# The end of a cached-attention layer: one head's PV moved behind half of the last pair's PV, and two runs of matmuls rolled into loops

## The chip, the core and the metric

The kernel runs on one core of one Trainium2 chip. The metric is the device time of one execution in microseconds (us). The core has a matrix engine (PE, with its weight loads shown as PEld), a vector engine (DVE), an activation engine (ACT), GpSimd (POOL) and an engine that here only starts transfers (SP). Each engine works through its own list of instructions in order; they meet at semaphores.

## The reference, cut to what matters

Two equal layers follow each other for one new token of a batch of two. Each is an attention over a cache of 16384 positions in 32 heads, and then a small MLP:

```python
def _A_ref(x, k_cache, v_cache, wq, wo):          # caches: 2 x 32 x 16384 x 128, bf16
    q = (x @ wq) split into 32 heads of 128
    scores = einsum("bhqd,bhkd->bhqk", q, k_cache) * 128 ** -0.5
    o = einsum("bhqk,bhkd->bhqd", softmax(scores), v_cache)
    return o, heads side by side, @ wo            # wo: 4096 x 576
def _B_ref(x, w1, w2, w3, w4):                    # x: 2 x 1 x 576
    ...
    h2 = gelu(layernorm(x1) @ w3) @ w4            # w3: 576 x 4608, w4: 4608 x 576
x = x + _A_ref(layernorm(x), ...); x = x + _B_ref(layernorm(x), ...)      # twice
```

K and V of one batch element and head ("head" below; there are 64) are 4 MB each.

## The kernel before, in words

**Memory and transfers.** One SBUF array `mem` is cut into six slots of 32 KB per partition. `plan_all` writes down every transfer in the order in which SP starts them; `Store.pump` lets a transfer start only when the last reader of its place is done. Transfers are planned far ahead, so a long queue of them stands in front of the DMA engines.

**Attention.** Heads go in pairs (`pair`, `pair_end`): PE transposes half of K (L1324) and multiplies it by q (L1335), ACT copies the transposes (L1425), DVE does the other half of K by products and sums (L1347, L1350); then the maximum over all partitions on POOL (L1371), the exponentials on ACT, and the product of the probabilities with V, "PV", on PE: 256 matmuls of one 128-wide block each (L1402). The pairs of a layer run in a loop of the program on PE, ACT and DVE; a place that changes by turn (which slot K lies in) is addressed through a register, and a register instruction stands ahead of each transpose (L1324). Each loop's body is built to start at the head of a block of instructions (`head_slot`).

**Layer 1's end** (`attention`, its last branch). One single head `c` is left after the pairs, and the last pair's PV. In order: `q_row` and `single` (K of `c`: L1309, L1435 on PE, L1446 and L1449 on DVE), `softmax_max` (DVE, then POOL's reduction over the partitions, L1464), `softmax_exp` (ACT, L1474 and L1478), `pv` of `c` (128 matmuls, L1511, into column 448 of the PSUM tile `mps`, copied out by ACT, L1493). Then the last pair's PV in four quarters (`pv_pair_part`, L1402) into the same two columns; its V comes in two transfers of 4 MB, one for quarters 0 and 1, one for 2 and 3. Between the halves stands `totals` (L1231: sums over the softmax denominators). `weighted` (L1063) and a fold by PE (L1022) turn all heads' outputs into the operand of wo.

**Landings.** `landed` puts an item in POOL's list that waits for a transfer and then raises a semaphore that PE waits on. POOL works through its list in order, and the same list holds the reductions.

**After attention.** `rows_projection` multiplies by wo (32 rows of 5 matmuls in three pieces of 11, 11 and 10 rows, L924), then layernorms, w3 (L800, L817), gelu, w4 (L924 again, six pieces), and the output. SP's queue after the last pair's V holds, in this order, wo, w3, w4 and w1. Part of w4 goes to the slot in which V of head `c` lies.

Of the kernel before, what the change touches and what calls it, by code (L numbers as in the profile page):

```python
# [4 lines left out]
ACT = mybir.ActivationFunctionType  # L5
# [337 lines left out]
class KB:  # L343
# [346 lines left out]
    def layer(self, l):  # L690
        if l == 0:
            self.unscaled()
        self.q_projection(l)
        if l == 0:
            self.hs_projection()
            self.quads()
        self.attention(l)
        ot = self.otn.rearrange("p (b j) -> p j b", b=self.B)
        self.rows_projection("wo", l, lambda k: ot[:, k, :], "prod")
        self.add_psum(self.x, "x", self.x, "x", self.unscaled)  # L700
        self.layernorm("x", self.x, self.xb, "xb")
        self.dv(lambda e: e.tensor_copy(out=self.mean0[:, :], in_=self.mv[:, 0, :]), reads=["mv"], writes=["mean0"])
        self.dv(lambda e: e.tensor_copy(out=self.rstd0[:, :], in_=self.rstd[:, :]), reads=["rstd"], writes=["rstd0"])
        self.dv(lambda e: e.tensor_tensor(out=self.x1[:, :, :], in0=self.xb[:, :, :], in1=self.hs[:, :, :],
                                          op=ALU.add), reads=["xb", "hs"], writes=["x1"])
        self.z_projection(l)
        if l == 0:
            self.turn(1, settle=False)
        self.gelu_z()
        self.settle()  # L710
        self.rows_projection("w4", l, lambda k: self.gT[:, k * self.B:(k + 1) * self.B], "prod")
        self.dv(lambda e: e.tensor_tensor(out=self.x[:, :, :], in0=self.x[:, :, :], in1=self.x1[:, :, :],
                                          op=ALU.add), reads=["x", "x1"], writes=["x"])
        if l < self.NL - 1:
            self.add_psum(self.x, "x", self.x, "x", self.unscaled)
        else:
            self.dv(lambda e: e.tensor_tensor(out=self.xo[:, :, :], in0=self.x[:, :, :],
                                              in1=self.mps[:, 0:self.KT * self.B].rearrange("p (t b) -> p t b", b=self.B),
                                              op=ALU.add),
                    reads=["mps", "x"], writes=["xo"])  # L720
# [190 lines left out]
    def rows_projection(self, w, l, rhs, rk):  # L911

        KT, B, D = self.KT, self.B, self.D
        cuts = self.cuts[w, l]
        last = cuts[-1][1] - 1
        for i, (a, b, _) in enumerate(cuts):
            nm = (w, l, i)
            buf = self.store.buf(nm)

            def f(pe, a=a, b=b, buf=buf):  # L920
                for k in range(a, b):
                    for t in range(KT):
                        o = (k - a) * D + self.kcol[t]
                        ins = pe.matmul(self.mps[:, t * B:(t + 1) * B], lhsT=buf[:, o:o + 128], rhs=rhs(k),  # L924
                                        start=(k == 0 and t == 0), stop=(k == last), skip_group_check=True)
                return ins
            self.pe(f, reads=[rk] + self.store.keys(nm), writes=["mps"])
            self.store.release(nm)
            if (w, i) == ("w4", 2 - l):
                self.layernorm("xb", self.xb, self.xn2[:, l, :, :], "xn2", bank=self.BANK)  # L930
                if l == self.NL - 1:
                    self.gelu(self.eps, "eps", self.junk, "junk")
            if l == 0:
                self.turn(self.TURNS.get((w, i), 0))
# [38 lines left out]
    def attention(self, l):  # L973
        o = self.order(l)
        n = self.PAIRS[l]
        at = lambda i: 2 * i - 1 if l == 0 else 2 * i + 1
        self.l_now = l
        if l:
            self.carried(o)
        else:  # L980
            self.q_row(o[0], 0, 2)
            self.q_turn(o[1], None)
            self.single(o[0], 0, 2)
            self.softmax_max(o[0], 0, 2)
            self.softmax_exp(o[0], 0, 2)
            self.pv(l, o[0], 0)
        self.pair(l, o[at(1)], 0, None, 2 * l)
        first = self.g.mark()
        first.pop("vector")
        self.base = self.chunk  # L990
        self.pair_end(o[at(1)], o[at(2)])
        sums = self.g.mark()["vector"]
        for i in range(2, n):
            self.pair(l, o[at(i)], (i - 1) % 2, o[at(i - 1)])
            self.pair_end(o[at(i)], o[at(i + 1)])
        self.g.loop({"vector": sums}, n - 2)
        last = o[at(n)]
        self.pair(l, last, (n - 1) % 2, o[at(n - 1)])
        self.g.loop(first, n - 1)
        self.base = None  # L1000
        self.pair_end(last)
        c = o[-1]
        if l == 0:
            self.last_three(last, *o[-3:])
        else:
            self.q_row(c, 0, 2)
            self.single(c, 0, 2)
            self.softmax_max(c, 0, 2)
            self.softmax_exp(c, 0, 2)
            self.pv(l, c, 0)  # L1010
            self.landed("vp", last, apart=True)
            for g in range(4):
                if g == 2:
                    self.totals(l)
                self.pv_pair_part(l, last, g)
            for h in range(2):
                self.weighted(last + h, self.mps[:, 448 + h:449 + h])
        t = self.sps[self.BANK][:, self.U:2 * self.U]

        def f(pe):  # L1020
            for b in range(self.B):
                ins = pe.matmul(t[:, 32 * b:32 * b + 32], lhsT=self.spread[:, 128 * b:128 * (b + 1)],  # L1022
                                rhs=self.fold[:, :], start=True, stop=True, skip_group_check=True)
            return ins
        self.pe(f, reads=["prod", "fold"], writes=[("sps", self.BANK)])
        self.dv(lambda e: e.tensor_copy(out=self.otn, in_=t), reads=[("sps", self.BANK)], writes=["prod"])
# [456 lines left out]
                                            bias=self.ls[:, 1, z:z + 1]),  # L1483
                     reads=[("ls0", z), ("ls1", z)], writes=[("l", u)])

    def pv(self, l, u, z, land=True):

        if land:
            self.landed("v", u)
        n = self.BP // 2  # L1490
        for b in range(0, self.NB, n):
            self.pv_part(l, u, z, b, b + n)
        self.act(lambda e: e.activation(out=self.o_acc[:, u:u + 1], in_=self.mps[:, 448:449], func=ACT.Copy),  # L1493
                 reads=["ops"], writes=[("o", u)])

    def pv_part(self, l, u, z, b, end):

        p = self.p[z]
        runs = []
        while b < end:  # L1500
            nm = next(x for x in self.store.pieces("v", u) if x[2] <= b < x[2] + x[3])
            m = min(end, nm[2] + nm[3]) - b
            runs.append((b, m, *self.tile("v", u, b, m)))
            b += m
        keys = [k for r in runs for k in r[4]]

        def f(pe):
            for b0, m, _, buf, _ in runs:
                for j in range(m):
                    b = b0 + j  # L1510
                    ins = pe.matmul(self.mps[:, 448:449], lhsT=buf[:, j * 128:(j + 1) * 128], rhs=p[:, b:b + 1],  # L1511
                                    start=b == 0, stop=b == self.NB - 1, skip_group_check=True)
            return ins
        self.pe(f, reads=[("p", z), ("p2", z)] + [("landed", r[2]) for r in runs] + keys, writes=["ops"])
        for _, m, nm, _, _ in runs:
            self.used(l, nm, m)

# [92 lines left out]
```

## Time and profile before

| | us |
|---|---|
| median of 3 runs | 2540.45 (2539.97 to 2540.72) |
| the profiled execution's own time | 2540.23 |
| its span, first to last instruction | 2538.4 |
| busy: PE / PEld / DVE / ACT / POOL | 1621.6 / 1478.7 / 1881.7 / 1255.4 / 30.8 |
| read from HBM | 1091.46 MB, 430 GB/s over the span |

Times in a profile count from the span's start; 1.83 us of the execution's time lie outside the span. A row of the timeline gives start, duration, engine, line of the kernel, operation, output and inputs with their shapes, how many such instructions follow each other, and in brackets how long the engine stood idle before and what ended that. "issue" means that it waited for nothing that the profile shows. PEq, PEldq, DVEq and SPq are the engines' sequencers, which run register and branch instructions and start transfers.

### The profile page before, as it was taken

To read this page: it belongs to the slowest core of one execution; us is meant where nothing else is said; L and a number is where in the kernel's file an instruction comes from. 1 tells how busy PE (TensorE), PEld (TensorE's weight loads), DVE (VectorE), ACT (ScalarE), POOL (GpSimd) and SP (SyncE) were. 2 spreads that over 40 slices of the span, in tenths; PEclk is the share of its full clock that TensorE was granted. 3 is DMA by queue.
4 is the path that set the end of the run, shared out by engine and by line. 5 is a ranking of instruction groups with operands and counts; after the bars stand their busy time and mean duration, and the time that the engine had idled before them with its cause. 6 is when DMAs were issued, how large, how long until landed. Compare 5 with 4: busy or idle time off the path is not lost.

```text
span 2538.4 us, 82111 instructions
## 1 busy us (share of the span) xinstructions
PE 1621.6 (64%) x34342; PEld 1478.7 (58%) x34342; DVE 1881.7 (74%) x1549; ACT 1255.4 (49%) x1940; POOL 30.8 (1%) x94
## 2 busy tenths in 40 slices
PE   3665665666666666657667765666566666656666
PEld 3555655565556556556656655565566556555655
DVE  5877787787787777777648877877778778778773
ACT  2545545445446455455435564454554544644542
POOL 0000000000000000000000000000000000000000
PEclk8666666666666666666656666666666666666665
DMA  9999999999999999999999999999999999999999
GB/s 413 431 435 433 433 435 433 433 433 437 432 434 432 438 430 435 433 433 434 414 411 418 430 430 443 432 431 430 443 432 430 431 439 435 431 431 436 438 423 395
DMA packets 30226, 1092.31 MB, mean 430 GB/s; under 512 B 3284, under 2 KB 4440, under 8 KB 10840
## 3 DMA queue, kind: packets, MB, share of 16 engines
q1 hardware_dynamic: 30168, 1091.47, 99.8%
q8 instruction: 45, 0.74, 0.1%
q14 instruction: 13, 0.11, 0.0%
HBM read 1091.46 MB, written 0.00 MB: 430 GB/s over the span
## 4 chain that ended last, share of the span: by engine, by line
DMA 76%; PE 18%; issue 3%; ACT 1%; SPq 1%; DVE 0%; ACTq 0%; POOLq 0%; POOL 0%; DVEq 0%
DMA mem<-in_A_v_cache_dram 73%; PE mps L1402 16%; DMA mem<-in_B_w_dram 1%; DMA mem<-in_A_k_cache_dram 1%; PE mps L1511 1%; ACT kt L1425 1%; SPq L101 1%; ACT o_acc L1411 0%; PE tps L1324 0%; DMA mem<-in_A_wo_dram 0%; DMA mem<-in_A_wq_dram 0%; PE mps L924 0%; PE mps L1435 0%; PE tps L1435 0%; PE tps L1309 0%
## 5 line engine op out<-in xcount | busy, mean ns | idle before, releaser
L1324 PE MATMUL tps<-same,mem 128*128 128x128 bf16 x7680 | 951.0, 268 | 253.1 <-POOLq L206 251.3
L1350 DVE TENSOR_REDUCE s_dve<-prod 128x16 f32<-128x2048 bf16 x480 | 1097.4, 2286 | 16.5
L1425 ACT ACTIVATE kt<-tps 128x1024 bf16<-128x1024 bf16 x985 | 993.1, 1028 | 197.3 <-PE tps L1324 174.9
L1324 PEld LDWEIGHTS tps<-same,mem 128*128 (+1 forms) x7680 | 707.8, 112 | 364.0 <-issue 254.1
L1347 DVE TENSOR_TENSOR prod<-mem,qb 128x2048 bf16<-128x2048 bf16 x480 | 587.9, 1225 | 344.9 <-POOLq L206 280.0
L1402 PE MATMUL mps<-both,mem 128*128 128x2 bf16 x15360 | 420.2, 165 | 435.4 <-POOLq L206 421.1
L1402 PEld LDWEIGHTS mps<-both,mem 128*128 128x128 bf16 x15360 | 415.0, 103 | 441.0 <-POOLq L206 426.2
L1411 ACT ACTIVATE o_acc<-mps 128x2 f32 (+1 forms) x59 | 10.2, 174 | 792.5 <-PE mps L1402 792.5
L1335 PE MATMUL sps<-q_pair,kt 128*128 128x2 bf16 x7680 | 347.9, 167 | 49.9 <-ACT kt L1425 46.7
L1335 PEld LDWEIGHTS sps<-q_pair,kt 128*128 128x128 bf16 x7680 | 327.9, 104 | 62.0 <-ACT kt L1425 60.8
L1366 DVE TENSOR_REDUCE mq<-sps 64x1 f32<-64x128 f32 x120 | 34.6, 288 | 165.3 <-PE sps L1335 163.4
L1273 ACT ACTIVATE qb<-sps 128x128 bf16<-128x128 f32 x66 | 18.3, 278 | 141.4 <-PE sps L1269 141.3
L1269 PE MATMUL sps<-same,q_pair 128*64 128x128 bf16 x120 | 17.9, 294 | 82.3 <-DVE q_pair L1282 77.5
L1269 PEld LDWEIGHTS sps<-same,q_pair 128*64 128x64 bf16 x120 | 7.5, 121 | 87.5 <-DVE q_pair L1282 82.7
L1449 DVE TENSOR_REDUCE s_dve<-prod 128x16 f32<-128x2048 bf16 x24 | 54.9, 2286 | 0.8
L1309 PE MATMUL tps<-same,mem 128*128 128x128 bf16 x432 | 45.4, 279 | 7.9 <-POOLq L206 5.0
L1380 ACT ACTIVATE both<-s_dve,mq 64x128 bf16<-64x128 f32 x120 | 48.0, 400 | 2.2
L1371 POOL PARTITION_ALL_REDUCE mq<-mq x60 | 21.4, 357 | 2268.5 <-DVE mq L1369 2268.5
L1511 PE MATMUL mps<-p,mem 128*128 128x1 bf16 x1024 | 29.6, 165 | 28.9 <-ACT p L1478 18.6
L1446 DVE TENSOR_TENSOR prod<-mem,qb 128x2048 bf16<-128x2048 bf16 x24 | 29.4, 1224 | 24.0 <-DMA mem<-in_A_k_cache_dram 14.3
L1511 PEld LDWEIGHTS mps<-p,mem 128*128 128x128 bf16 x1024 | 28.5, 104 | 30.1 <-ACT p L1478 19.0
L1384 ACT ACTIVATE both<-sps,mq 64x128 bf16<-64x128 f32 x120 | 43.7, 364 | 3.0
(148 smaller groups left out, 454.8 us busy)
## 6 DMA issues: line engine op xcount, KB each, us to landing
mem<-in_A_k_cache_dram SPq DMA_DIRECT2D x9, 4096.0 KB, 30.0
mem<-in_A_v_cache_dram SPq DMA_DIRECT2D x6, 4096.0 KB, 30.8
mem<-in_B_w_dram SPq DMA_DIRECT2D x21, 576.0 KB, 7.7
mem<-in_B_w_dram SPq DMA_DIRECT2D x7, 1152.0 KB, 35.9
mem<-in_A_wq_dram SPq DMA_DIRECT2D x10, 512.0 KB, 6.5
mem<-in_A_wo_dram SPq DMA_DIRECT2D x8, 576.0 KB, 17.7
mem<-in_A_wq_dram SPq DMA_DIRECT2D x4, 1024.0 KB, 8.1
mem<-in_A_k_cache_dram SPq DMA_DIRECT2D x4, 1024.0 KB, 10.8
```

The source lines that it names most:

```text
L1309: ins = pe.transpose(to[:, j * 128:(j + 1) * 128], buf[:, j * 128:(j + 1) * 128], self.ident[:, :])
L1324: ins = pe.transpose(self.tps[t][:, j * 128:(j + 1) * 128], self.mem[:, bass.ds(base + (c * self.CH + j) * 128, 128)], self.ident[:, :])
L1335: ins = pe.matmul(self.sps[1][:, i:i + 2], lhsT=buf[:, j * 128:(j + 1) * 128], rhs=self.q_pair[:, :], start=True, stop=True, skip_group_ch ...
L1347: self.dv(lambda e, base: e.tensor_tensor(out=prod, in0=self.mem[:, bass.ds(base + b * 128, DB * 128)].rearrange("p (j d) -> p j d", d=128 ...
L1350: self.dv(lambda e: e.tensor_reduce(out=self.s_dve[2][:, d * DB:(d + 1) * DB], in_=prod, axis=AX.X, op=ALU.add), reads=["prod"], writes=[( ...
L1366: self.dv(lambda e, h=h, r=r: e.tensor_reduce(out=m[r, 1:2], in_=self.pair_scored(r, h), axis=AX.X, op=ALU.max), reads=[("sps", 1)], write ...
L1380: self.act(lambda e, h=h, r=r: e.activation(out=self.both[r, h, n:2 * n], in_=self.s_dve[2][r, :], func=ACT.Exp, bias=m[r, 6:7], scale=sel ...
L1384: self.act(lambda e, h=h, r=r: e.activation(out=self.both[r, h, 0:n], in_=self.pair_scored(r, h), func=ACT.Exp, bias=m[r, 6:7], scale=self ...
L1402: ins = pe.matmul(self.mps[:, 448:450], lhsT=buf[:, at:at + 128], rhs=self.both[:, :, b], start=b == 0, stop=b == 2 * self.NB - 1, skip_gr ...
L1425: self.act(lambda e: e.activation(out=out, in_=src, func=ACT.Copy), reads=[key], writes=keys, sig=("evac", key, keys[0]))
L1449: self.dv(lambda e: e.tensor_reduce(out=self.s_dve[z][:, d * DB:(d + 1) * DB], in_=prod, axis=AX.X, op=ALU.add), reads=["prod"], writes=[( ...
L1511: ins = pe.matmul(self.mps[:, 448:449], lhsT=buf[:, j * 128:(j + 1) * 128], rhs=p[:, b:b + 1], start=b == 0, stop=b == self.NB - 1, skip_g ...
```

## The change

In layer 1's last branch, the two halves of the last pair's PV now stand on either side of the PV of head `c`: quarters 0 and 1, then `pv` of `c`, then `totals`, then quarters 2 and 3. Since the pair's sums stay in column 448 of `mps` meanwhile, the PV of `c` gets another place, column 448 of the PSUM tile `sps0` (`apart_place`). The three `landed` items (V of `c`, and both halves of the last pair's V) move ahead of `softmax_max`, and so ahead of its reduction in POOL's list.

The PV of `c` and, in layer 1, wo now run as loops of the program on PE. `blocks` runs 8 matmuls written out, 7 turns of 16 in a loop, and 8 written out; both operands, the block of V and the column of `p`, are addressed through registers. wo's pieces run one row (5 matmuls) written out, 4 turns of two rows, and the remaining rows written out, three times over; there the weights' place is computed for every matmul, and the operand's column once a row.

```diff
-        self.rows_projection("wo", l, lambda k: ot[:, k, :], "prod")
+        self.rows_projection("wo", l, lambda k: ot[:, bass.ds(k, 1), :].rearrange("p o b -> p (o b)"), "prod")
...
+            def g(pe, a=a, b=b, home=home):
+                row = lambda k, x, inner=False: [pe.matmul(
+                    self.mps[:, t * B:(t + 1) * B], lhsT=self.mem[:, bass.ds(x + self.kcol[t], 128)], rhs=rhs(k),
+                    start=not inner and (k == 0 and t == 0), stop=not inner and k == last, skip_group_check=True)
+                    for t in range(KT)][-1]
+                n, me = 2, pe.engine
+                snap = lambda x: self.nc.snap(x, engines=OrderedEngineSet([me]))
+                turns = (b - a - 2) // n
+                row(a, home + a * D)
+                with self.nc.Fori(0, turns, 1, engines=OrderedEngineSet([me]), head_slot={me: 0}) as turn:
+                    at, k0 = snap(turn * (n * D) + home + (a + 1) * D), snap(turn * n + a + 1)
+                    for j in range(n):
+                        row(k0 + j, at + j * D, True)
+                for k in range(a + 1 + n * turns, b):
+                    ins = row(k, home + k * D)
+                return ins
+            self.pe(g if (w, l) == ("wo", 1) else f, reads=[rk] + self.store.keys(nm), writes=["mps"])
...
             self.single(c, 0, 2)
+            self.landed("v", c)
+            self.landed("vp", last, apart=True)
             self.softmax_max(c, 0, 2)
             self.softmax_exp(c, 0, 2)
-            self.pv(l, c, 0)
-            self.landed("vp", last, apart=True)
             for g in range(4):
                 if g == 2:
+                    self.pv(l, c, 0, False, looped=True, apart=True)
                     self.totals(l)
                 self.pv_pair_part(l, last, g)
...
+    def apart_place(self):
+
+        return self.sps[0][:, 448:449], ("sps", 0)
+
+    def blocks(self, pe, b0, m, one):
+
+        head, n = 8, 16
+        turns = (m - 2 * head) // n
+        if turns < 2:
+            head, turns = m, 0
+        for b in range(b0, b0 + head):
+            ins = one(b)
+        if turns:
+            me = pe.engine
+            with self.nc.Fori(0, turns, 1, engines=OrderedEngineSet([me]), head_slot={me: 0}) as turn:
+                first = self.nc.snap(turn * n + b0 + head, engines=OrderedEngineSet([me]))
+                at = self.nc.snap(turn * (n * 128) + (b0 + head) * 128, engines=OrderedEngineSet([me]))
+                for j in range(n):
+                    one(first + j, at + j * 128, True)
+            for b in range(b0 + head + n * turns, b0 + m):
+                ins = one(b)
+        return ins
```

On PE, from the PV of head `c` to the last pair's second half, before (L1511 is the PV of `c`, L1402 the pair's, L1231 `totals`):

```order
L1511 MATMUL mps<-p,mem 128x1 [waits landed_tensor_tensor,done_scalar]
L1511 MATMUL mps<-p,mem 128x1 x127
L1402 MATMUL mps<-both,mem 128x2 [waits done_scalar,landed_tensor_tensor]
L1402 MATMUL mps<-both,mem 128x2 x127
L1231 MATMUL sps<-l,ones_f 128x64
L1402 MATMUL mps<-both,mem 128x2 [waits landed_tensor_tensor]
L1402 MATMUL mps<-both,mem 128x2 x127
```

The same place now (the pair's PV is L1421; L1529 sets up and turns the loop, L1559 is the PV of `c`; an ISA row is a register instruction, or the alignment of the loop's head):

```order
L1421 MATMUL mps<-both,mem 128x2 [waits landed_tensor_tensor]
L1421 MATMUL mps<-both,mem 128x2 x127
L1559 MATMUL sps<-p,mem 128x1 [waits done_scalar]
L1559 MATMUL sps<-p,mem 128x1 x7
L1529 ISA
L1529 UNCONDITIONAL_BRANCH
L1529 ISA
L1559 ISA
L1559 MATMUL sps<-p,mem 128x1
L1559 ISA
L1559 MATMUL sps<-p,mem 128x1
L1559 ISA
```

The first half of the pair's PV has moved ahead; of the 128 matmuls of `c`, 112 now have a register instruction in front of them, and a jump stands ahead of the loop.

On PE, the multiplication by wo, before:

```order
L924 MATMUL mps<-prod,mem 128x2 [waits wo0,done_vector]
L924 MATMUL mps<-prod,mem 128x2 x54
L924 MATMUL mps<-prod,mem 128x2 [waits wo1]
L924 MATMUL mps<-prod,mem 128x2 x54
L924 MATMUL mps<-prod,mem 128x2 [waits wo2]
L924 MATMUL mps<-prod,mem 128x2 x49
```

The same place now, from its first matmul into the first of three loops (L938 is the loop, L930 its matmuls):

```order
L930 MATMUL mps<-prod,mem 128x2 [waits wo0,done_vector]
L930 MATMUL mps<-prod,mem 128x2 x4
L938 ISA
L938 UNCONDITIONAL_BRANCH
L938 ISA
L930 ISA
L930 MATMUL mps<-prod,mem 128x2
L930 ISA
L930 MATMUL mps<-prod,mem 128x2
```

Of 160 matmuls, 120 now have a register instruction in front of them, and there are three loops, each with a jump ahead of it.

On POOL, the end of its list with the semaphores waited for, before (L1371 are the pairs' reductions, L1464 that of head `c`; `tile0` is K of `c`, `tile1` its V, `part4_0` and `part4_128` are the halves of the last pair's V):

```order
L1371 ISA mq<-mq 128x2 [waits pair2,pair4,done_vector]
L1371 ISA mq<-mq 128x2 [waits pair0,pair4,done_vector]
L1371 ISA mq<-mq 128x2 [waits pair2,pair4,done_vector]
L1464 ISA mx<-mx 128x1 [waits tile0,done_vector]
L232 UNCONDITIONAL_BRANCH [waits tile1,part4_0,part4_128]
```

And now:

```order
L1390 ISA mq<-mq 128x2 [waits pair2,pair4,done_vector]
L1390 ISA mq<-mq 128x2 [waits pair0,pair4,done_vector]
L1390 ISA mq<-mq 128x2 [waits pair2,pair4,done_vector]
L1483 ISA mx<-mx 128x1 [waits tile0,tile1,part4_0,part4_128,done_vector]
L232 UNCONDITIONAL_BRANCH
```

The reduction of head `c` now stands behind the landings of its V and of both halves of the last pair's V.

More of the change, by code (lines that the diff above doesn't have):

```diff
@@ L926, in f @@
                 return ins
-            self.pe(f, reads=[rk] + self.store.keys(nm), writes=["mps"])
+            home = self.store.where[nm][0] // 2 - a * D
+            def g(pe, a=a, b=b, home=home):
[15 more added lines that the diff above has]
+            self.pe(g if (w, l) == ("wo", 1) else f, reads=[rk] + self.store.keys(nm), writes=["mps"])
             self.store.release(nm)
@@ L1484, in softmax_exp, with pv, pv_part @@
                      reads=[("ls0", z), ("ls1", z)], writes=[("l", u)])
-    def pv(self, l, u, z, land=True):
+    def pv(self, l, u, z, land=True, looped=False, apart=False):
         if land:
             self.landed("v", u)
-        n = self.BP // 2
+        n = self.NB if looped else self.BP // 2
         for b in range(0, self.NB, n):
[L1492 to L1496, printed above, removed]
+            self.pv_part(l, u, z, b, b + n, looped, apart)
+        out, key = self.apart_place() if apart else (self.mps[:, 448:449], "ops")
+        self.act(lambda e: e.activation(out=self.o_acc[:, u:u + 1], in_=out, func=ACT.Copy), reads=[key], writes=[("o", u)])
+    def apart_place(self):
[17 more added lines that the diff above has]
+        return ins
+    def pv_part(self, l, u, z, b, end, looped=False, apart=False):
         p = self.p[z]
+        out, key = self.apart_place() if apart else (self.mps[:, 448:449], "ops")
         runs = []
@@ L1505, in pv_part, with g @@
         keys = [k for r in runs for k in r[4]]
+        rows = []
+        for b0, m, nm, *_ in runs:
+            home = self.store.where[nm][0] // 2 - 128 * nm[2]
+            if rows and rows[-1][2] == home:
+                rows[-1][1] += m
+            else:
+                rows.append([b0, m, home])
+        def g(pe):
+            for b0, m, home in rows:
+                ins = self.blocks(pe, b0, m, lambda c, x=None, inner=False, home=home: pe.matmul(
+                    out, lhsT=self.mem[:, bass.ds((c * 128 if x is None else x) + home, 128)],
+                    rhs=p[:, bass.ds(c, 1)], start=not inner and c == 0, stop=not inner and c == self.NB - 1,
+                    skip_group_check=True))
+            return ins
         def f(pe):
@@ L1510, in f @@
                     b = b0 + j
-                    ins = pe.matmul(self.mps[:, 448:449], lhsT=buf[:, j * 128:(j + 1) * 128], rhs=p[:, b:b + 1],
+                    ins = pe.matmul(out, lhsT=buf[:, j * 128:(j + 1) * 128], rhs=p[:, b:b + 1],
                                     start=b == 0, stop=b == self.NB - 1, skip_group_check=True)
             return ins
-        self.pe(f, reads=[("p", z), ("p2", z)] + [("landed", r[2]) for r in runs] + keys, writes=["ops"])
+        self.pe(g if looped else f, reads=[("p", z), ("p2", z)] + [("landed", r[2]) for r in runs] + keys, writes=[key])
         for _, m, nm, _, _ in runs:
```

## The prediction

> **What bounds the kernel now.** First the page, its chain of work that ended last:
>
> ```profile
> span 2538.4 us, 82111 instructions
> DMA 76%; PE 18%; issue 3%; ACT 1%; SPq 1%; DVE 0%; ACTq 0%; POOLq 0%; POOL 0%; DVEq 0%
> ```
>
> The kernel is a stream of transfers. The change touches only layer 1's end, so next the same chain in order of time, its last part:
>
> ```profile
> 2514.95 20.05 DMA mem<-in_B_w_dram
> 2535.00 0.05 issue
> 2535.05 0.44 PE mps L924 x10
> ```
>
> The last piece of w4 lands at 2535.0, and the span ends 3.4 us later. How far is PE from that? Its timeline on w4:
>
> ```profile
> 2527.46 2.29 PE L924 MATMUL mps<-prod,mem 128*128 128x2 bf16 x80 [0.62 <-ACT prod L967]
> ...
> 2531.30 2.11 PE L924 MATMUL mps<-prod,mem 128*128 128x2 bf16 x70 [1.12 <-DMA mem<-in_B_w_dram]
> 2534.19 0.69 PE L924 MATMUL mps<-prod,mem 128*128 128x2 bf16 x20 [0.78 <-DMA mem<-in_B_w_dram]
> 2535.05 0.42 PE L924 MATMUL mps<-prod,mem 128*128 128x2 bf16 x10 [0.16 <-DMA mem<-in_B_w_dram]
> ```
>
> PE waits for w4 three times, 1.12 + 0.78 + 0.16 = 2.06 us. So PE has about 2 us to spare at the end and no more: whatever makes it quicker is lost in these waits, and whatever makes it slower by over 2 us is paid in full. Where the change acts:
>
> ```profile
> 2493.66 3.58 PE L1511 MATMUL mps<-p,mem 128*128 128x1 bf16 x128 [8.55 <-ACT p L1478]
> 2497.59 1.66 PE L1402 MATMUL mps<-both,mem 128*128 128x2 bf16 x57 [0.35 <-ACT o_acc L1493]
> 2500.80 2.05 PE L1402 MATMUL mps<-both,mem 128*128 128x2 bf16 x71 [1.55 <-issue]
> 2502.72 0.67 PE L1231 MATMUL sps<-l,ones_f 128*128 128x64 f32 x2
> 2503.18 1.65 PE L1402 MATMUL mps<-both,mem 128*128 128x2 bf16 x55
> 2507.01 2.11 PE L1402 MATMUL mps<-both,mem 128*128 128x2 bf16 x73 [2.17 <-issue]
> ...
> 2510.12 1.54 PE L924 MATMUL mps<-prod,mem 128*128 128x2 bf16 x52 [0.32 <-DVE prod L1026]
> 2513.07 3.02 PE L924 MATMUL mps<-prod,mem 128*128 128x2 bf16 x108 [1.41 <-issue]
> ```
>
> A matmul written out costs 3.58 / 128 = 0.028 us. The stalls put down to issue end at 2500.80, 2507.01 and 2513.07, 6.1 to 6.2 us apart, and between them lie 71 + 2 + 55 = 128 and 73 + 2 + 52 = 127 matmuls. I read that as PE's instructions arriving in blocks of some 128 matmuls, one per 6.2 us, the next asked for when the present one is entered. These three stalls, 5.13 us, and the 8.55 us of waiting are what the change can win.
>
> The Trainium skill ("Runtime: NRT & Kernel Launch", section "Instruction fetch mechanics") has instructions come in blocks of 16 KiB, 256 instructions, the crossing "mostly hidden"; the block's size agrees with these rows (a matmul and its weight load are two), the hiding does not.
>
> **Step 1, the reduction on POOL.**
>
> ```profile
> 2492.24 0.37 POOL L1464 PARTITION_ALL_REDUCE mx<-mx  x1 [18.47 <-DVE mx L1462]
> ```
>
> The landings of the last pair's V, from the transfers SP started around 2466:
>
> ```profile
> L101 SPq DMA_DIRECT2D mem<-in_A_v_cache_dram x2: 327/380/433, 2466.2 to 2466.6; - x2
> ...
> DMA to landing us min/median/max: 22.0/26.7/31.4
> ```
>
> The halves land at 2466.2 + 22.0 = 2488.2 and 2466.6 + 31.4 = 2498.0. POOL's list now has both landings ahead of this reduction, which so moves from 2492.24 to 2498.0. Queued behind it are the exponentials on ACT and PE's PV of `c`, which followed it by 2493.66 - 2492.24 = 1.42: it can start at 2499.4. Meanwhile the pair's first half runs from 2488.2 to about 2492, in what was idle time: its 3.7 us leave the path, and the 1.55 us stall inside it too.
>
> **Step 2, the PV of `c` as a loop.** 112 matmuls get a register instruction each. The trace has such a loop, L1324, beside the same transposes written out, L1309:
>
> ```profile
> 2401.03 3.25 PE L1324 MATMUL tps<-same,mem 128*128 128x128 bf16 x24 [4.69 <-POOLq L206]
> ```
> ```profile
> 2473.44 2.31 PE L1309 MATMUL tps<-same,mem 128*128 128x128 bf16 x24 [0.54 <-POOLq L206]
> ```
> ```profile
> L1324 PE MATMUL tps<-same,mem x131: 216/283/314, 2401.0 to 2440.0; 128*128 128x128 bf16 x131
> L1324 PEldq FUSED_REGOPS  x129: 46/46/46, 2401.1 to 2439.9; - x129
> ```
>
> 24 start in 3.25 - 0.28 us: 0.129 us from one to the next, of which the register instruction is 0.046. Written out it is at most 2.31 / 24 = 0.096. A PV matmul, with 1 column instead of 128, is ready every 0.028, so in a loop the register instruction and the way to its weight load set the pace. That is the cheap end, 0.129. But here each register instruction forms two addresses (sum, product, sum, twice), L1324's only one. Rows for longer ones:
>
> ```profile
> L271 PEldq FUSED_REGOPS  x58: 172/173/207, 77.3 to 2439.5; - x58
> ```
> ```profile
> L1282 DVEq FUSED_REGOPS  x56: 75/75/75, 116.9 to 2434.5; - x56
> ```
> ```profile
> L1347 DVEq FUSED_REGOPS  x392: 57/57/65, 81.9 to 2427.0; - x196
> ```
>
> On DVE four steps take 75 ns and three 57, 18 a step; PE's three take 46 for DVE's 57, so some 14 a step, and six steps 88. L271 has six with a remainder among them and takes 173: the dear end. I take 88, since ours have sums and products only: 0.129 + 0.042 = 0.171 us a matmul (0.129 to 0.256). A turn adds:
>
> ```profile
> L261 PEldq COMPARE_BRANCH  x60: 76/208/4868, 73.0 to 2472.5; - x60
> ...
> L261 PEldq ALU_OP  x58: 36/36/42, 116.3 to 2472.4; - x58
> ```
>
> 208 + 36, and a register instruction of seven steps at its head, nearest to L271's 173: with a little for dispatch 0.5 us (0.25 to 0.5). Sum: 112 x 0.171 + 7 x 0.5 + 16 x 0.028 + 0.2 for the jump = 23.3 us (16.8 to 32.8), where it took 3.58. The PV of `c` ends at 2522.7.
>
> The w4 pieces that wait for V of `c`'s slot go out then:
>
> ```profile
> 2499.47 8.14 SPq L101 DMA_DIRECT2D mem<-in_B_w_dram  x1
> ```
> ```profile
> DMA to landing us min/median/max: 29.0/29.0/29.0
> ```
>
> That one landed at 2528.5 after waiting its turn in a full queue. At 2522.7 there is still work queued for about 5 us, and PE comes to w4 much later (step 5): nothing.
>
> **Step 3, totals and the second half.** 0.67 + 128 x 0.028 = 4.3 us, to 2527.0, without stall since the loop gave the next block time. The fold as before, 2510.12 - (2507.01 + 2.11) = 1.0: wo begins at 2528.0.
>
> **Step 4, wo.** Each loop's head starts a block, so PE must have that block before it jumps. What an entry can cost stands at the pair loop of layer 1:
>
> ```profile
> 1365.28 0.32 PE L1269 MATMUL sps<-same,q_pair 128*64 128x128 bf16 x2 [4.78 <-issue]
> ```
>
> The PV loop's code, its 8 last matmuls, `totals` and 92 of the second half's 128 matmuls fill one block. The one after it is entered 36 x 0.028 = 1.0 before the second half's end, at 2526.0; the next comes 6.2 later, at 2532.2, and PE is at the jump at 2528.2: 4.0 us lost (0 to 4.8). The two later loops have theirs in time, as each takes over 6.2 us. Twelve turns of 8 x 0.129 + 2 x 0.171 + 0.5 = 1.87 are 22.5; with 40 matmuls written out and jumps 24 us (20 to 26), where wo took 5.97. wo ends at 2556.2, before at 2513.07 + 3.02 = 2516.1: 40.1 us late.
>
> **Step 5, the rest.** From wo's end to the span's were 2538.4 - 2516.1 = 22.3, 2.06 of it waits for w4, which has now all landed: 20.2. Span 2576.4; with the 1.83 us outside it (2540.23 - 2538.4) **2578.2**, 38 us over the profiled execution, which lies 0.2 under the median of the runs. With all cheap ends (-6.5, -4.0, -4.0) 2563.7; with all dear ones (+9.5, +0.8, +2.0) 2590.5.
>
> **Rivals.**
> *Register work hidden.* If PE's sequencer ran far enough ahead, looped matmuls would go at 0.028. Then PV of `c` ends at 2503, wo at about 2513, PE meets w4 earlier and waits longer for it; the last landing at 2535.0 sets the end: **2540**, no change. For it: L1324's matmuls may be held by the transposes themselves. Against: the same transposes take 0.096 at most when written out, so it is the register instruction that holds the loop at 0.129, though the sequencer had every chance to run ahead. 6%.
> *Only the cheap ends.* Two addresses cost as much as one, and wo's first jump finds its block: **2564**. 15%.
> *The dear ends.* **2590**. 8%.
> *Every back edge fetches its block.* Fifteen taken back edges (6 and 3 x 3) at 4.78 would add 72 us: **2650**. Against: the pair loop turns at a median of 0.208, and its body is far over two blocks. 1%. The skill's same section says that a taken branch to outside a window of two blocks forces a fetch, and so prefers unrolled code; by that the pair loop too would stall each turn, and its row shows it does not, but the advice speaks against this change.
> *Faster.* The stalls that go are worth 5 us of PE, but its waits for w4 already swallow 2 and would swallow the rest. For a gain of over 5 us the last landing would have to come earlier, to **2535** or less for the whole, and the change alters no transfer. 1%.
>
> **How the numbers follow.** The forecast has 69%. The range runs from a little under the cheap ends to a little over the dear ones, 2562 to 2592, and leaves out the first rival, the back edges and the gain. About 0.2%, 5 us, is what a measurement can tell from no change: slower 93%, the same 6%, faster 1%.
>
> **What would show it.** Right: POOL's last reduction at about 2498; 128 pair matmuls from 2488; the looped matmuls 0.13 to 0.26 apart; PV of `c` over 17 us; an idle time put down to issue ahead of wo's first loop; wo over 20 us; no wait for w4 left. Wrong: looped matmuls at 0.03, or PE still waiting for w4 at the end.

## The result, and the profile after

The changed kernel took 2575.19 us in the median of 4 runs (2575.07 to 2577.36), the kernel before, beside it, 2540.21 (2539.44 to 2540.72). The ratio is 1.0141, 95% interval 1.0126 to 1.0156: slower by 35.0 us. 2578.2 was predicted, 2562 to 2592.

The page of the changed kernel: the span and its chain.

```profile
span 2573.4 us, 82407 instructions
...
DMA 73%; PE 20%; issue 3%; ACT 2%; DVE 2%; SPq 0%; POOL 0%; POOLq 0%; ACTq 0%; DVEq 0%
```

The span grew by 35.0 us, all of the difference. DMA's share of the chain fell from 76% to 73%: a stretch at the end no longer belongs to the transfers. POOL's last reduction, from the timeline:

```profile
2496.68 0.37 POOL L1483 PARTITION_ALL_REDUCE mx<-mx  x1 [24.07 <-DMA mem<-in_A_v_cache_dram]
```

It waits for a transfer now, and runs 4.4 us later than before (2496.68 against 2492.24). PE's timeline over layer 1's end:

```profile
2486.87 3.57 PE L1421 MATMUL mps<-both,mem 128*128 128x2 bf16 x128 [3.17 <-POOLq L206]
2498.11 0.37 PE L1559 MATMUL sps<-p,mem 128*128 128x1 bf16 x8 [7.67 <-ACT p L1497]
2499.04 2.58 PE L1559 MATMUL sps<-p,mem 128*128 x16 [0.56 <-issue]
...
2514.69 2.53 PE L1559 MATMUL sps<-p,mem 128*128 x16 [0.56 <-issue]
2517.78 2.96 PE L1559 MATMUL sps<-p,mem 128*128 x24 [0.56 <-issue]
2520.60 0.67 PE L1250 MATMUL sps<-l,ones_f 128*128 128x64 f32 x2
2521.06 3.60 PE L1421 MATMUL mps<-both,mem 128*128 128x2 bf16 x128
...
2525.67 0.29 PE L930 MATMUL mps<-prod,mem 128*128 128x2 bf16 x5 [0.32 <-DVE prod L1045]
2529.58 1.43 PE L930 MATMUL mps<-prod,mem 128*128 x10 [3.62 <-issue]
2531.58 1.36 PE L930 MATMUL mps<-prod,mem 128*128 x10 [0.57 <-issue]
2533.51 1.36 PE L930 MATMUL mps<-prod,mem 128*128 x10 [0.57 <-issue]
2535.54 1.98 PE L930 MATMUL mps<-prod,mem 128*128 x25 [0.66 <-issue]
2537.83 1.39 PE L930 MATMUL mps<-prod,mem 128*128 x10 [0.31 <-issue]
...
2552.02 1.75 PE L930 MATMUL mps<-prod,mem 128*128 x15 [0.56 <-issue]
...
2565.10 2.29 PE L924 MATMUL mps<-prod,mem 128*128 128x2 bf16 x80 [0.62 <-ACT prod L985]
2567.26 0.57 PE L743 MATMUL sps<-misc,ones_f 128*128 128x4 f32 x2
2567.68 2.81 PE L924 MATMUL mps<-prod,mem 128*128 128x2 bf16 x100
```

The first half of the pair's PV moved into idle time, and no stall is left in either half. But the PV of head `c`, 3.58 us before, goes from 2498.11 to 2517.78 + 2.96 = 2520.74, 22.6 us, in groups of 16 with 0.56 to 0.61 us between them. wo, 5.97 us before, goes from 2525.67 to 2553.77, 28.1 us, with 3.62 us of waiting ahead of its first loop. w4 runs without a wait for a transfer: the three waits of before are gone, since everything has landed. The instructions by line, weight loads and sequencer of PE (nanoseconds: least, median, most):

```profile
L1559 PEldq FUSED_REGOPS  x112: 69/74/88, 2498.9 to 2520.0; - x112
```
```profile
L930 PEldq FUSED_REGOPS  x120: 46/46/79, 2529.5 to 2553.1; - x120
```
```profile
L938 PEldq COMPARE_BRANCH  x15: 76/214/3394, 2525.8 to 2553.3; - x15
L938 PEldq FUSED_REGOPS  x12: 170/175/175, 2529.2 to 2551.7; - x12
```
```profile
L1529 PEldq COMPARE_BRANCH  x8: 76/212/400, 2498.2 to 2520.2; - x8
```

There is one register instruction per looped matmul, 74 ns for two addresses, 46 for one. Of wo's 15 branches three are the jumps to its loops: the first took 3394 ns, the longest of all, and the two later ones 292 and 288. The jump to the PV's loop took 400. The back edges that were taken, nine here and six in the PV's loop, took 207 to 228 ns each.

### The profile page after: what moved, and what is told of

Read it like the earlier page. It is cut to its first block, busy times and chain, and to the rows that moved or that the text cites. A ratio compares the mean times of both kernels' runs of the same rounds, so it can differ in the third digit from the quotient of the medians.

```text
span 2573.4 us, 82407 instructions
## 1 busy us (share of the span) xinstructions
PE 1648.9 (64%) x34342; PEld 1492.5 (58%) x34342; DVE 1881.5 (73%) x1549; ACT 1251.2 (49%) x1940; POOL 30.7 (1%) x94
## 4 chain that ended last, share of the span: by engine, by line
DMA 73%; PE 20%; issue 3%; ACT 2%; DVE 2%; SPq 0%; POOL 0%; POOLq 0%; ACTq 0%; DVEq 0%
DMA mem<-in_A_v_cache_dram 71%; PE mps L1421 16%; DMA mem<-in_A_k_cache_dram 1%; ACT kt L1444 1%; PE sps L1559 1%; DVE s_dve L1468 1%; PE mps L1569 1%; PE mps L930 1%; DMA mem<-in_B_w_dram 1%; PE tps L1343 0%; ACT o_acc L1430 0%; DVE prod L1465 0%; PE mps L924 0%; PE tps L1328 0%; DMA mem<-in_A_wo_dram 0%
## 5 line engine op out<-in xcount | busy, mean ns | idle before, releaser
L1421 PE MATMUL mps<-both,mem 128*128 128x2 bf16 x15360 | 420.0, 165 | 432.9 <-POOLq L206 422.9
L1421 PEld LDWEIGHTS mps<-both,mem 128*128 128x128 bf16 x15360 | 414.9, 103 | 438.5 <-POOLq L206 428.2
L1328 PEld LDWEIGHTS tps<-same,mem 128*128 128x128 bf16 x432 | 35.9, 125 | 9.5 <-POOLq L206 4.8
## 6 DMA issues: line engine op xcount, KB each, us to landing
mem<-in_A_v_cache_dram SPq DMA_DIRECT2D x6, 4096.0 KB, 30.8
```

Source lines behind the costliest of these rows:

```text
L1328: ins = pe.transpose(to[:, j * 128:(j + 1) * 128], buf[:, j * 128:(j + 1) * 128], self.ident[:, :])
L1421: ins = pe.matmul(self.mps[:, 448:450], lhsT=buf[:, at:at + 128], rhs=self.both[:, :, b], start=b == 0, stop=b == 2 * self.NB - 1, skip_gr ...
```

## The experiments

The theory is the prediction's: looped matmuls go at the pace of their register instructions, turns add to that, and one loop's entry waits for code; order and landings cost nothing at the end. Rival A: the reduction behind the landings costs the time. Rival B: the jumps and new blocks of code starve PE. "Before" in each comparison is the kernel before, on the same chip.

**The order without the loops.**

```diff
-            self.pe(g if (w, l) == ("wo", 1) else f, reads=...
+            self.pe(f, reads=...
...
-                    self.pv(l, c, 0, False, looped=True, apart=True)
+                    self.pv(l, c, 0, False, apart=True)
```

> The new order, place and landings, with the PV of head c and wo written out as before. Theory (the price is the register instructions of the loops, their turns and one entry; order and landings hide under the transfers): PE ends the pair's second half at about 2506 to 2508 and waits for w4 at the end, 2540, within 0.2% of the kernel before. Rival A (the reduction that now waits for the last pair's V is what costs): its 4 to 6 us delay reaches the end, 2544 to 2546. Rival B (the new blocks of code and jumps starve PE): no jumps here, so 2540 too.

Measured: 2539.98 us beside 2539.77, ratio 1.0002 (0.9993 to 1.0011). PE's timeline of this kernel:

```profile
2488.88 3.57 PE L1421 MATMUL mps<-both,mem 128*128 128x2 bf16 x128 [3.34 <-POOLq L206]
2500.14 3.57 PE L1569 MATMUL sps<-p,mem 128*128 128x1 bf16 x128 [7.69 <-ACT p L1497]
...
2507.16 2.08 PE L1421 MATMUL mps<-both,mem 128*128 128x2 bf16 x72 [1.45 <-issue]
...
2531.26 2.29 PE L924 MATMUL mps<-prod,mem 128*128 128x2 bf16 x70 [0.95 <-DMA mem<-in_B_w_dram]
```

The pair's PV ends at 2509.24, before at 2509.12: what the first half gains by moving, the delayed reduction takes back, even on PE. That balance goes by the execution: SP started the last pair's V at 2466.7 here, at 2465.0 in the changed kernel's trace. The waits for w4 stay (0.95, 0.66 and 0.20 us). Rival A is out as the cause of 35 us: with the same order and landings the time is that of before.

**Each loop alone.** The first keeps the loop of the PV of `c` and writes wo out (the first edit above), the second the other way round (the second edit).

> The new order with the PV of head c in its loop, wo written out. Theory: PV still takes 22 to 23 us and ends the second half at about 2524.7 as in the changed kernel; wo then takes 4.6 to 6 instead of 28, so 22 to 23 us less than the changed kernel: 2552 to 2553. Rival A: near 2545. Rival B (entries starve PE): this loop's entry showed no long stall, so it should give nearly the time of the kernel before, 2540 to 2543.

> The new order with wo in its three loops, the PV of head c written out. Theory: wo begins at 2507 to 2509 and takes 24 to 28 us, ends at 2533 to 2537 instead of 2553.8: 17 to 21 us less than the changed kernel, 2554 to 2558. Rival A: near 2545. Rival B: wo's three entries are the price, 2570 or more.

Measured: 2552.76 us with the PV's loop, ratio 1.0051 (1.0035 to 1.0066), and 2557.57 with wo's loops, 1.0071 (1.0055 to 1.0086), both beside 2539.77. wo written out, in the first:

```profile
2525.83 2.56 PE L924 MATMUL mps<-prod,mem 128*128 128x2 bf16 x90 [0.32 <-DVE prod L1045]
2529.38 2.02 PE L924 MATMUL mps<-prod,mem 128*128 128x2 bf16 x70 [1.00 <-issue]
```

And the start of wo in the second:

```profile
2508.18 0.29 PE L930 MATMUL mps<-prod,mem 128*128 128x2 bf16 x5 [0.32 <-DVE prod L1045]
```

13.0 and 17.8 us more than before. In the first, wo ends at 2531.40, 15.3 after that of before (2516.09), and the span is 12.7 longer (2551.1 against 2538.4): 2.6 us are forgiven. Where, the kernel before shows:

```profile
2519.27 0.91 PE L800 MATMUL sps<-misc,mem 128*128 128x7 bf16 x18 [0.47 <-issue]
2520.40 0.59 PE L743 MATMUL mps<-misc,ones_f 128*128 128x4 f32 x2 [0.22 <-DVE misc L740]
...
2529.61 0.57 PE L743 MATMUL sps<-misc,ones_f 128*128 128x4 f32 x2
```

From the last of these rows to the end of w4 are 2535.05 + 0.42 - 2529.61 = 5.86 us, with the three waits between. In the changed kernel the same stretch takes 2567.68 + 2.81 - 2567.26 = 3.23, and in this run as long: 2.63 less. The waits as the timeline counts them are 2.06 of it; the rest is that w4's matmuls, run in one piece, overlap where the pieces could not. The stall of 0.47 us among w3's matmuls goes too, but wins nothing, since PE then waits for DVE instead: from wo's end to the second L743 behind it are 2520.40 - 2516.09 = 4.31 us before and 4.30 in this run. The allowance is given once, so the two prices add to less (30.8) than both loops cost together (35.0). It explains 2.6 of these 4.2 us. In both of these traces the transfers were as early as in the changed kernel's (within 0.2 us); with the PV written out, wo then begins at 2508.18, 1.9 us earlier than in the kernel before, and such a lead too can be given only once. This is about the size of the rest, but no run separates it. Rival B fails on the first: a loop whose entry showed only 0.56 us costs 13.

**Both loops in the old order.**

```diff
-            self.landed("v", c)
-            self.landed("vp", last, apart=True)
             self.softmax_max(c, 0, 2)
             self.softmax_exp(c, 0, 2)
+            self.pv(l, c, 0, looped=True)
+            self.landed("vp", last, apart=True)
             for g in range(4):
                 if g == 2:
-                    self.pv(l, c, 0, False, looped=True, apart=True)
                     self.totals(l)
```

> Both loops, but the old order, place and landings: PV of head c first, then the whole of the last pair's PV. Theory: PV of c starts 5 to 6 us earlier and the pair's first half comes after it, 3.6 us; 0 to 2 us less than the changed kernel, 2573 to 2576. Rival A (order and landings cost the time): back to 2540 to 2546.

Measured: 2575.82 us beside 2539.77, ratio 1.0145 (1.0130 to 1.0161), which can't be told from the changed kernel's 1.0141. Its PE timeline:

```profile
2492.28 0.37 PE L1558 MATMUL mps<-p,mem 128*128 128x1 bf16 x8 [8.78 <-ACT p L1496]
...
2515.25 3.56 PE L1420 MATMUL mps<-both,mem 128*128 128x2 bf16 x128 [0.35 <-ACT o_acc L1512]
...
2523.22 1.12 PE L1420 MATMUL mps<-both,mem 128*128 128x2 bf16 x36 [1.46 <-issue]
...
2529.80 1.41 PE L930 MATMUL mps<-prod,mem 128*128 x10 [4.16 <-issue]
```

The PV of `c` starts 5.8 us earlier than in the changed kernel. The pair's first half, back on the path, takes 3.6 of it, a stall comes back with 1.46, and wo's entry waits 0.5 longer. So the order is worth nothing here either way.

**One address instead of two.** Each looped matmul of the PV takes the same column of `p`.

```diff
-                    rhs=p[:, bass.ds(c, 1)], start=...
+                    rhs=p[:, 8:9] if inner else p[:, bass.ds(c, 1)], start=...
```

> The changed kernel, but every looped matmul of the PV of head c takes the same column of p (the other columns of the loop are left out of the sum), so that its register instruction forms one address instead of two. Theory (the register instruction sets the pace of a looped matmul): it shrinks from 74 to 46 ns and the pace from 0.157 to about 0.128 us, 112 x 0.029 = 3.2 us less than the changed kernel: 2571.5 to 2572.5. Rival (the pace is that of a weight load or matmul with an address in a register): no change, 2575.

Measured: 2571.91 us beside 2540.04, ratio 1.0126 (1.0111 to 1.0142); 31.9 us over before instead of 35.0. Its register instructions and a turn:

```profile
L1559 PEldq FUSED_REGOPS  x105: 46/46/46, 2499.5 to 2517.1; - x105
```
```profile
2510.10 2.11 PE L1559 MATMUL sps<-p,mem 128*128 128x1 bf16 x16 [0.53 <-issue]
2512.70 2.10 PE L1559 MATMUL sps<-p,mem 128*128 128x1 bf16 x16 [0.49 <-issue]
```

There are 105 of them and not 112, as the head of the loop now forms the address of each turn's first matmul. The register instruction fell from 74 to 46 ns, the pace from (2.53 - 0.18) / 15 = 0.157 us to (2.11 - 0.18) / 15 = 0.129, by the same 28 ns (0.18 is the matmul's own duration). From its end to the start of the weight load are 0.05 us in both traces, so nothing else in the step changed. The register instruction sets the pace.

**wo's loops without a block of their own.**

```diff
-                with self.nc.Fori(0, turns, 1, engines=OrderedEngineSet([me]), head_slot={me: 0}) as turn:
+                with self.nc.Fori(0, turns, 1, engines=OrderedEngineSet([me])) as turn:
```

> The changed kernel, but wo's three loops don't ask for their head at a block's start; the loop of the PV of head c still does. Theory (the 3.6 us ahead of wo's first loop are the wait for the block that its head opens): the first loop lies in the block PE is in already, 3 to 3.6 us less: 2571.5 to 2572.5. Rival (a jump or a loop entry costs that wherever it goes): 2575. A third way, that a loop across a block's end fetches at each turn: 2580 or more.

Measured: 2570.99 us beside 2540.04, ratio 1.0124 (1.0109 to 1.0139). Its wo:

```profile
2525.73 0.29 PE L930 MATMUL mps<-prod,mem 128*128 128x2 bf16 x5 [0.32 <-DVE prod L1045]
2526.19 1.40 PE L930 MATMUL mps<-prod,mem 128*128 x10 [0.17 <-issue]
2528.17 1.36 PE L930 MATMUL mps<-prod,mem 128*128 x10 [0.58 <-issue]
...
2532.12 3.33 PE L930 MATMUL mps<-prod,mem 128*128 x35 [0.57 <-issue]
2536.02 1.36 PE L930 MATMUL mps<-prod,mem 128*128 x10 [0.57 <-issue]
```

The wait ahead of the first loop is 0.17 instead of 3.62, and the turns are as they were. It is 4.0 us less than the changed kernel over before, a little past the 3 to 3.6 that were expected, and more than the first entry's 3.62 - 0.17 = 3.45 us. The rest comes from the other two entries, which had not been counted: from the last turn of the first loop to the second turn of the second are 2539.84 - 2535.54 = 4.30 us in the changed kernel and 2536.02 - 2532.12 = 3.90 here, and 0.47 us go in the same way at the third. That makes 4.3 us, as the two profiled executions differ (2575.15 and 2570.86). The trace has 12 branches at L938 where there were 15: the jumps ahead of the loops are gone with the alignment. That the jump by itself is not the price of the first entry is seen in the changed kernel, where the other three took 0.29 to 0.40 us.

**Fewer, longer turns.**

```diff
-        head, n = 8, 16
+        head, n = 8, 56
```

> The changed kernel, but the loop of the PV of head c runs 2 turns of 56 matmuls instead of 7 of 16. Theory (a turn adds some 0.6 us, a matmul 0.157): 5 turns less are 3 us; the longer body also fills its block sooner, so that the block of wo's first loop is asked for up to 1.7 us earlier: 2570 to 2572.5. Rival (turns cost only their branch, 0.2 us): 2574.

Measured: 2570.76 us beside 2540.04, ratio 1.0121 (1.0106 to 1.0137). Its PE timeline:

```profile
2497.97 0.37 PE L1559 MATMUL sps<-p,mem 128*128 128x1 bf16 x8 [7.68 <-ACT p L1497]
2498.91 8.94 PE L1559 MATMUL sps<-p,mem 128*128 x56 [0.56 <-issue]
2508.41 9.22 PE L1559 MATMUL sps<-p,mem 128*128 x64 [0.57 <-issue]
...
2524.95 1.40 PE L930 MATMUL mps<-prod,mem 128*128 x10 [2.10 <-issue]
```

The gap between turns is the same 0.57, and five of them are gone: the PV of `c` takes 2508.41 + 9.22 - 2497.97 = 19.66 us instead of 22.63, 3.0 less. wo's entry waits 2.10 instead of 3.62, 1.5 less. Together that is the gain, 4.3 us between the medians (2575.19 - 2540.21 against 2570.76 - 2540.04), within a few tenths.

**The order with the landings put right, no loops.** The first half's landing stays ahead of the reduction, the second half's goes behind it, on top of the first experiment.

```diff
             self.landed("v", c)
-            self.landed("vp", last, apart=True)
+            self.landed_part("vp", last, 0)
             self.softmax_max(c, 0, 2)
+            self.landed_part("vp", last, 1)
             self.softmax_exp(c, 0, 2)
```

> The new order and place without loops, and the landing of the last pair's second half behind the reduction of head c in POOL's list, the first half's ahead of it. Theory: the reduction runs at about 2490 to 2492 again, PE ends wo 3 to 6 us earlier than in the kernel before, and all of that is lost in longer waits for w4: 2539.5 to 2540.5, within 0.2% of the kernel before. Rival (PE bounds this end, and the new order frees it): 2535 to 2537.

Measured: 2539.51 us beside 2540.04, ratio 0.9999 (0.9990 to 1.0008). Its PE timeline:

```profile
2492.27 3.79 PE L1575 MATMUL sps<-p,mem 128*128 128x1 bf16 x128 [2.05 <-ACT p L1503]
...
2508.56 1.50 PE L924 MATMUL mps<-prod,mem 128*128 128x2 bf16 x50 [0.60 <-DMA mem<-in_A_wo_dram]
...
2530.57 2.14 PE L924 MATMUL mps<-prod,mem 128*128 128x2 bf16 x70 [1.86 <-DMA mem<-in_B_w_dram]
2533.75 1.11 PE L924 MATMUL mps<-prod,mem 128*128 128x2 bf16 x30 [1.03 <-DMA mem<-in_B_w_dram]
```

wo ends at 2510.06, 6.0 us before that of the kernel before, and now PE waits for transfers from wo on. The end does not move. This is the order that the change was after, at its best, and the transfers take all of it.

## Why the prediction was right, step by step

| step | predicted, us | the changed kernel, us |
|---|---|---|
| reduction on POOL at | 2498.0 | 2496.68 |
| from it to the PV of `c` | 1.42 | 1.43 |
| PV of `c` | 23.3 | 22.6 |
| to wo's start | 5.3 | 4.9 |
| wait ahead of wo's first loop | 4.0 | 3.62 |
| wo with that wait | 28.2 | 28.1 |
| from wo's end to the span's | 20.2 | 19.6 |
| span | 2576.4 | 2573.4 |

- *What bounds the kernel.* Shown from both sides: PE 6.0 us earlier changes nothing, PE later is paid but for 2.6 us.
- *Step 1.* The mechanism was right. The time was 1.3 us early because the transfers were that much ahead in this execution: SP started this V at 2465.0 where it was 2466.2 before, and the pair's first half, which starts at its landing, began at 2486.87, where 2488.2 was read from before. Over the traces with the new order that start lies between 2486.64 and 2488.88, so these 1.3 us are chance.
- *Step 2.* The pace was set between two rows and came out nearer to the cheap one: 0.157 us, with the register instruction at 74 ns for six steps where 88 was taken and 46 and 173 were the ends. A step so costs some 9 ns, (74 - 46) / 3, where 14 was taken. A turn added 3.09 - 16 x 0.157 = 0.58 for 0.5, and 0.5 was the upper end of what was allowed for it. The two errors cancel in part: 22.6 for 23.3. The one-address experiment shows that the pace is the register instruction's.
- *Step 3.* No stall in the second half, as said.
- *Step 4.* Turn of wo 2533.51 - 2531.58 = 1.93 us, 1.87 predicted. That wo comes out at 28.1 for 28.2 is partly luck: the first entry was 0.4 us cheaper than said, turns and later entries 0.3 dearer. The entry's wait came from the block that the loop's head opens: without `head_slot` it is gone. Its size fits the blocks as counted: 92 matmuls into the second half, at 2521.06 + 92 x 0.028 = 2523.6, the block before is entered, and 6.2 us later, at 2529.8, the next was due; the loop's first matmul ran at 2529.58. The Trainium skill ("Runtime: NRT & Kernel Launch", section "Instruction fetch mechanics") would have unrolled code preferred because a taken branch can leave the window of fetched code. The trace has such a wait at this one forward jump, 3394 ns. The back edges here, over 10 and 16 matmuls, took 207 to 228 ns without one, and most of the price, registers and turns, is not in that rule.
- *Step 5.* The waits for w4 went, as said. They were taken off at 2.06 us, the idle time in the timeline; with the overlap of the matmuls that they had kept apart they were worth 2.63, and so the rest is 19.6 and not 20.2.
- *The rivals.* Hidden register work is refuted by the 28 ns that both rows of the one-address experiment moved. The cheap ends fail on the 74 ns and on the wait of 3.62 us, the dear ends on the 74 ns where 173 would have been needed. Fetching at each back edge would have shown in 15 branches; none of them took over 228 ns, and the one branch that waited is a jump into a loop.

In all, order and landings are 0 us. Of the 35.0 us, the three single edits put back 3.1 (one address), 4.0 (wo's entries) and 4.3 (five turns, with an earlier entry). The larger part, looped matmuls at 0.129 us and up where written ones take 0.028, was not taken out by an edit of its own, only with its loop. By the rows it is 112 x (0.157 - 0.028) = 14.4 us in the PV and 120 x (0.129 - 0.028) = 12.1 in wo, an estimate of PE's time before the 2.6 us are forgiven.

## What to carry to other kernels

Before short matmuls are rolled into a loop to save code, compare the pace of one written out with the pace that a loop of the same kernel shows for an instruction addressed through a register; here that is 0.028 against 0.129 to 0.157 us, and rolling up 112 + 120 = 232 matmuls cost 35 us, while the stalls that went with it were 1.4 to 2.2 us each. Ask first whether the engine bounds its stretch at all: in the last 50 us of a stream of transfers, 6 us of PE time were worth nothing. And an item that only waits, put into an engine's list early, holds up everything behind it in that list: here a reduction by 4.4 us, which only the transfers hid.

## What the runs showed of the hardware that was not expected

- A register instruction on PE that forms two addresses (six steps) took 74 ns, one that forms one (three) 46: by these two about 9 ns a step, an estimate.
- Between two turns of a loop PE stood idle 0.56 to 0.67 us, at 10, 16 and 56 matmuls a turn (0.49 to 0.55 with one address). In the first turn of the PV's loop in the changed kernel this is the branch (0.23, partly under the last matmul), the register instruction at the loop's head (0.175) and that of the first matmul (0.07), with 0.05 to 0.06 between one and the next.
- The wait ahead of the same loop changed with the code ahead of it: 3.62 us in the changed kernel, 4.16 in the old order, 2.10 with the longer body of the PV's loop ahead of it, and 0.17 where the head opens no block.
